# Attention and a gated two-layer product on one core: offsets for the first three chunks, 16 float32 heads instead of 24, the weights' checks near the end, the gate written over h

## The chip, the cores and the metric

The kernel runs on one core of a Trainium2 chip. The metric is the time of one execution on the device in microseconds (us); lower is better. PE is TensorE, which multiplies matrices; DVE (VectorE), ACT (ScalarE) and POOL (GpSimd) work element by element; SP issues the DMA transfers. PSUM is the memory that PE writes, in banks of 128 x 512 float32 values; SBUF is the other memory on the chip.

## What is computed

```python
# q, k, v: (4, 8, 768, 64) float32; n_sink = 4, window = 128
scores = (1 / sqrt(64)) * q @ k.T
keep = (pos_k < n_sink) | ((pos_q - pos_k >= 0) & (pos_q - pos_k < window))
scores = where(keep, scores, -1e9)
a = exp(scores - max(scores)); a = a / (sum(a) + 1e-9)
x = concat_heads(a @ v)                # 3072 x 512
h = x @ w_in                           # w_in 512 x 2048
out = (h * cos(h)) @ w_out             # w_out 2048 x 512, out 3072 x 512 float32
```

The two weights come as float64 arrays; everything else is float32. The inputs are random; q and k are scaled so that the softmax is sharp.

## The kernel before

**Tiles.** The 3072 rows are worked in 12 chunks of 256 rows: a chunk is one batch and two blocks of 128 positions, (batch, first block). Each chunk has 8 heads, and after them 8 slots. A slot takes 256 of the 2048 columns of h.

**Numbers in pieces.** A product of nearly float32 accuracy is made of three products of a shorter type (float32r): each operand is kept as a high part and a low rest, and hi*hi, lo*hi and hi*lo are summed in PSUM. The weights are turned from float64 into such pieces on the chip at the start (weight_piece: 32 pieces of 512 KB; three integer steps on DVE, L482, L488, L494, the high part on ACT, L515, the rest on DVE or POOL, L518).

**A slot** (dense): 24 h matmuls of 128 x 256 (L381) into one PSUM bank; then ACT scales h into an integer number of turns (L390), DVE takes the rest of the turn (L396, tile r), ACT the cosine (L403), DVE multiplies h and the cosine, the gate (L408, into r), ACT takes the high part ghi (L414) and DVE or POOL the low rest glo (L420). After that, 12 acc matmuls of 128 x 512 (L429) add the slot's part to the chunk's two output banks. After a chunk's last slot the output is copied through a raw buffer (L370, L372) and stored. r, ghi and glo have two buffers each; h goes round over the banks b4 and b2 in the first two chunks, and over b4, b2 and b3 from the third.

**A head.** The first NEH = 24 heads, three chunks of 8, are "early" and take the float32 path: q and k are loaded in natural order and turned on PE (L713), scores are float32 matmuls (L737), the values too (L925), and a small matmul (L327) takes the high part of x away again. The other heads take the split path: q and k are loaded in strips and turned on DVE (L695, L766), split by ACT and DVE or POOL (l: L753, L760; k: L778, L784), and scores (L793) and values (L949) are float32r matmuls. Both paths share the masks on DVE (L806), the exponent on ACT (L815), the denominator (L824, L825), the norm of p (L835 on DVE or POOL, L833 on ACT), and the turn of p on PE (L895) with its high and low part (L904, L911). Chunks that don't begin at block 0 also see the sink columns: they have 264 instead of 256 score columns and some extra small steps (L865, L867, L877). The early chunks are the first chunks of batches 0, 1 and 2, so with NEH = 24 the chunks come as (0,0), (1,0), (2,0), (0,2), (0,4), (1,2) and so on.

**Checks.** The integer steps hold only for weights that aren't tiny. So all 32 pieces are loaded again later (check_piece), and DVE takes the least square of each (L533); at the end one value, redo, decides whether a general path runs, which it doesn't here. A check shares the two buffers raw and the two buffers wt with the weights, and raw with the output copies. Before, each slot from the third chunk on adds one check, with a priority of CK = 27.4 us after the slot's time.

**What sets the order.** Every step is handed to a list scheduler (Plan.order), with its engine or engines, its model duration, what it needs, and a priority in us that comes from the time of its head or slot plus constants of the table C. The scheduler runs through model time and on each engine takes the ready step of the lowest priority; where a step may go to several engines, constants such as POOLPEN and POOLF weigh them. The result is a fixed order for each engine, written out in the program; nothing is decided on the chip. A buffer's next use waits for the users of its last one.

Of the kernel before, what the change touches and what calls it, by code (L numbers as in the profile page):

```python
# [172 lines left out]
def attn_moe_kernel(ctx, tc, q, k, v, n_sink, window, w_in, w_out, out):  # L173
# [232 lines left out]
    def gate(o):  # L406
        def fn(e):
            nc.vector.tensor_tensor(out=o.r, in0=o.h, in1=o.r, op=ALU.mult)  # L408
        return fn

    def g_hi(o):
        def fn(e):
# [1 line left out]
            nc.scalar.copy(out=o.ghi, in_=o.r)  # L414
        return fn

    def g_lo(o):
        def fn(e):
# [1 line left out]
            e.tensor_tensor(out=o.glo, in0=o.r, in1=f32(o.ghi), op=ALU.subtract)  # L420
# [123 lines left out]
    def dense(plan, x, a, s, t, T, w_in_ready, w_out_ready, acc_banks, h_bank):  # L544
# [8 lines left out]
        if True:  # L553
# [13 lines left out]
            a0 = add([("ACT", act(FG * NT, False))], turns(o), mm + [by], t + C["DM"] + 7.2)  # L567
            a2 = add([("DVE", dve(FG * NT))], rest(o), [a0, br], t + C["DM"] + 8.0)
# [1 line left out]
            a3 = add([("ACT", act(FG * NT) + 0.09)], cosine(o), [a2], t + C["DM"] + 8.9, table="sin")  # L570
            a4 = add([("DVE", dve(FG * NT))], gate(o), [a3], t + C["DM"] + 9.5)
# [840 lines left out]
```

## Time and profile before

| | |
|---|---|
| three runs | 771.24, 774.18, 778.17 us |
| median | 774.18 us |
| profiled execution, its own time | 773.9 us |
| its span in the trace | 772.1 us |
| mean granted PE clock | 0.993 |
| instructions | 15308 |
| DMA, the kernel's transfers | 70.43 MB, mean busy share of 16 engines 38.2% |

The profiled execution is 0.3 us from the median, and 1.8 us longer than its span. The prediction shows the lines of the page and of the trace. In them, "x" is a count; a chain row has start, duration and what ran; a group row has the line, engine, operation, tiles, shapes, then busy us, mean ns of one, and the idle time ahead of them with what ended it.

### The profile page before, as it was taken

To read this page: it belongs to the slowest core of one execution; us is meant where nothing else is said; L and a number is where in the kernel's file an instruction comes from. 1 tells how busy PE (TensorE), PEld (TensorE's weight loads), DVE (VectorE), ACT (ScalarE), POOL (GpSimd) and SP (SyncE) were. 2 spreads that over 40 slices of the span, in tenths; PEclk is the share of its full clock that TensorE was granted. 3 is DMA by queue.
4 is the path that set the end of the run, shared out by engine and by line. 5 is a ranking of instruction groups with operands and counts; after the bars stand their busy time and mean duration, and the time that the engine had idled before them with its cause. 6 is when DMAs were issued, how large, how long until landed. Compare 5 with 4: busy or idle time off the path is not lost.

```text
span 772.1 us, 15308 instructions
## 1 busy us (share of the span) xinstructions
PE 748.2 (97%) x4987; PEld 660.9 (86%) x4987; DVE 608.5 (79%) x1597; ACT 577.9 (75%) x1345; POOL 150.5 (19%) x233
## 2 busy tenths in 40 slices
PE   7899999999989999999999999999999999999996
PEld 6566777888978989888899999999999999999995
DVE  6868888778868889989989988888878988964432
ACT  2779796878868787787787887897798788784332
POOL 2122210100313432212234321210211221220000
PEclk9999999999999999999999999999999999999998
DMA  5655464332455366275367243232242233110000
GB/s 149 173 158 170 133 192 156 65 57 39 88 157 110 56 185 163 40 191 138 65 164 187 45 114 54 46 70 45 38 87 53 46 76 60 31 39 1 28 1 32
DMA packets 215673, 71.50 MB, mean 93 GB/s; under 512 B 204320, under 2 KB 204320, under 8 KB 215584
## 3 DMA queue, kind: packets, MB, share of 16 engines
q1 hardware_dynamic: 215584, 70.43, 38.2%
q8 instruction: 41, 0.67, 0.4%
q14 instruction: 48, 0.39, 0.2%
HBM read 64.10 MB, written 6.29 MB: 91 GB/s over the span
## 4 chain that ended last, share of the span: by engine, by line
PE 80%; DVE 7%; DMA 5%; ACT 4%; issue 2%; SPq 1%; DVEq 0%; ACTq 0%
PE h L381 31%; PE acc L429 29%; PE av L949 5%; PE tp L895 4%; PE s L793 4%; DMA raw<-in_moe_w_in_dram 3%; PE s L737 2%; PE av L925 2%; DMA xk<-in_k_dram 1%; ACT p L815 1%; PE gp L877 1%; DVE p L806 1%; DVE plo L911 1%; DVE r L396 1%; SPq L675 1%
## 5 line engine op out<-in xcount | busy, mean ns | idle before, releaser
L381 PE MATMUL h<-xhi,whi_in 128*128 128x256 f32 x768 | 224.0, 292 | 2.4 <-DVE r L408 2.4
L381 PE MATMUL h<-xlo,whi_in 128*128 128x256 f32 x768 | 217.2, 283 | 0.1
L381 PE MATMUL h<-xhi,wlo_in 128*128 128x256 f32 x768 | 216.9, 282 | 0.0
L381 PEld LDWEIGHTS h<-xhi,whi_in 128*128 128x128 f32 x768 | 145.8, 190 | 15.3 <-issue 4.5
L429 PE MATMUL acc<-whi_out,ghi 128*128 128x512 f32 x384 | 157.5, 410 | 0.0
L381 PEld LDWEIGHTS h<-xhi,wlo_in 128*128 128x128 f32 x768 | 146.1, 190 | 7.5
L429 PE MATMUL acc<-wlo_out,ghi 128*128 128x512 f32 x384 | 151.7, 395 | 0.0
L429 PE MATMUL acc<-whi_out,glo 128*128 128x512 f32 x384 | 150.5, 392 | 0.0
L381 PEld LDWEIGHTS h<-xlo,whi_in 128*128 128x128 f32 x768 | 145.8, 190 | 0.3 <-DVE xlo L337 0.3
L806 DVE CUSTOM_DVE_ANT_0 p<-s,mk 128x264 f32<-128x264 f32 (+1 forms) x192 | 76.8, 400 | 33.2 <-PE s L793 21.8
L815 ACT ACTIVATE p<-p,st 128x264 f32<-128x264 f32 (+1 forms) x192 | 93.4, 489 | 0.7
L403 ACT ACTIVATE r<-r,neg 128x512 f32<-128x512 f32 x96 | 69.0, 723 | 26.7 <-DVE r L396 24.3
L429 PEld LDWEIGHTS acc<-whi_out,glo 128*128 128x128 f32 x384 | 72.2, 188 | 16.5
L420 DVE TENSOR_TENSOR glo<-r,ghi 128x512 fp32r<-128x512 f32 x82 | 57.7, 703 | 31.3 <-ACT ghi L414 30.5
L414 ACT CAST ghi<-r 128x512 fp32r<-128x512 f32 x96 | 59.0, 615 | 30.0 <-PE acc L429 29.0
L429 PEld LDWEIGHTS acc<-whi_out,ghi 128*128 128x128 f32 x384 | 72.6, 189 | 5.0 <-issue 0.7
L429 PEld LDWEIGHTS acc<-wlo_out,ghi 128*128 128x128 f32 x384 | 73.0, 190 | 3.8 <-DVE wlo_out L518 0.3
L408 DVE TENSOR_TENSOR r<-h,r 128x512 f32<-128x512 f32 x96 | 65.2, 680 | 11.7 <-ACT r L403 11.4
L390 ACT ACTIVATE yt<-h 128x512 int32<-128x512 f32 x96 | 57.1, 595 | 18.1 <-PE h L381 16.0
L396 DVE SCALAR_TENSOR_TENSOR r<-h,yt 128x512 f32<-128x512 f32 x96 | 65.6, 683 | 5.4 <-ACT yt L390 4.0
L835 POOL TENSOR_SCALAR p<-p,st 128x264 f32<-128x264 f32 (+2 forms) x65 | 36.7, 576 | 156.3 <-DVE st L825 122.3
L848 POOL TENSOR_TENSOR vr<-v,vr 128x192 fp32r<-128x192 f32 (+1 forms) x59 | 34.9, 591 | 160.6 <-ACT vr L843 143.2
(128 smaller groups left out, 1392.8 us busy)
## 6 DMA issues: line engine op xcount, KB each, us to landing
raw<-in_moe_w_in_dram SPq DMA_DIRECT2D x32, 512.0 KB
raw<-in_moe_w_out_dram SPq DMA_DIRECT2D x32, 512.0 KB
xk<-in_k_dram SPq DMA_DIRECT2D x256, 48.0 KB
out_dram<-raw SPq DMA_DIRECT2D x24, 256.0 KB
v<-in_v_dram SPq DMA_DIRECT2D x64, 96.0 KB
xq<-in_q_dram SPq DMA_DIRECT2D x144, 32.0 KB
v<-in_v_dram SPq DMA_DIRECT2D x32, 64.0 KB
xq<-in_q_dram SPq DMA_DIRECT2D x24, 64.0 KB
```

What stands on the lines that cost most here:

```text
L381: nc.tensor.matmul(out=o.h[:, t, :], lhsT=w[:, c, fs], rhs=xx[:, c, :], start=(c == 0 and n == 0), stop=(c == NC - 1 and n == 2),)
L390: nc.scalar.activation(out=yt, in_=o.h, func=AF.Copy, scale=INV2PI, bias=0.25)
L396: nc.vector.scalar_tensor_tensor(out=o.r, in0=o.h, scalar=INV2PI, in1=yt, op0=ALU.mult, op1=ALU.subtract)
L403: nc.scalar.activation(out=o.r, in_=o.r, func=AF.Sin, scale=TWOPI_DOWN, bias=quarter)
L408: nc.vector.tensor_tensor(out=o.r, in0=o.h, in1=o.r, op=ALU.mult)
L414: nc.scalar.copy(out=o.ghi, in_=o.r)
L420: e.tensor_tensor(out=o.glo, in0=o.r, in1=f32(o.ghi), op=ALU.subtract)
L429: nc.tensor.matmul(out=x.acc[j], lhsT=gg[:, t, j * P : (j + 1) * P], rhs=w[:, f, :], start=(f == 0 and n == 0), stop=(f == NFT - 1 and n = ...
L806: nc.vector.tensor_tensor_reduce(out=o.p[:, j, :w], in0=o.s_ps[j][:, :w], in1=masks[min(o.i0 + j, 2)][:, :w], op0=ALU.add, op1=ALU.min, sc ...
L815: nc.scalar.activation(out=o.p[:, j, :w], in_=o.p[:, j, :w], func=AF.Exp, bias=o.lead.st[:, 0, o.nth, j : j + 1], scale=-1.0, accum_out=o. ...
L835: e.tensor_scalar(out=o.p[:, j, :w], in0=o.p[:, j, :w], scalar1=r, scalar2=1.0, op0=ALU.mult, op1=ALU.mult)
L949: nc.tensor.matmul(out=dst, lhsT=lhs, rhs=rhs, start=(n == 0), stop=(n == len(seq) - 1), skip_group_check=True)
```

## The change

Seven things change. The constants of C have new values (one line is shown). NEH is 16, so that the third chunk is now (0,2), on the split path and with sinks, and (2,0) comes later, on the split path too; with two early chunks the h banks are two in the first chunk only and three from the second. FIRST gives the steps of the first three chunks offsets of their own by kind of step (h, acc, the middle of a slot, q and k, scores, exponent, v, values), and the weights' pieces a shift by slot. The gate writes over h in PSUM, ghi and glo read it there, glo runs on DVE alone, r is free after the gate and the bank after glo. Checks are added so that they all end with the last slot: CR = 0.876 a slot in the last 8 slots, CS = 0.643 a slot before those. The idle matmuls that fill PE's waits at the start are 40 instead of 60. A minus of an odd head waits for the first part of its pair.

```diff
-    "DV": 4.41, "DX": 7.018, "FILL": 60, "GHI": 2, "GLO": 2, "L": 1, "LAG": 4.21, "LEAD": 18.263, "NEH": 24,
+    "LEAD": 24.62, "NEH": 16, "NM": 2.964, "NW": 2.34, "NWF": 0.132, "PB": 5, "PEN": 21.472, "PL": 3, "POOLF": 0.59,
...
+FIRST = {
+    "A": [-1.28, 4.17, 0.42], "H": [-6.37, 2.87, -2.13], "L": [-3.51, 18.2, 4.58], "M": [4.02, -1.74, 1.96],
...
+    def extra(kind, a):
+        return FIRST[kind][a] if a < 3 else 0.0
...
-            m = add([("PE", 0.11)], x_minus(x, p, odd), [i], t + 0.3)
+            m = add([("PE", 0.11)], x_minus(x, p, odd), [i] + (x.parts[p][:1] if odd else []), t + 0.3)
...
-            nc.vector.tensor_tensor(out=o.r, in0=o.h, in1=o.r, op=ALU.mult)
+            nc.vector.tensor_tensor(out=o.h, in0=o.h, in1=o.r, op=ALU.mult)
...
-            nc.scalar.copy(out=o.ghi, in_=o.r)
+            nc.scalar.copy(out=o.ghi, in_=o.h)
...
-            e.tensor_tensor(out=o.glo, in0=o.r, in1=f32(o.ghi), op=ALU.subtract)
+            e.tensor_tensor(out=o.glo, in0=o.h, in1=f32(o.ghi), op=ALU.subtract)
...
-            bh.users += [a0, a2, a4]
-            a5 = add([("ACT", act(FG * NT))], g_hi(o), [a4, bhi], t + C["DM"] + 10.2)
-            a6 = add(sub(FG * NT), g_lo(o), [a5, blo], t + C["DM"] + 10.8, port=True)
-            br.users += [a5, a6]
+            br.users.append(a4)
+            a5 = add([("ACT", act(FG * NT, False))], g_hi(o), [a4, bhi], tm + 10.2)
+            a6 = add([("DVE", dve(FG * NT))], g_lo(o), [a5, blo], tm + 10.8)
+            bh.users += [a0, a2, a4, a5, a6]
...
-            if a > 1 and len(checked) < len(checks):
+            left = len(slots) - nh
+            while len(checked) < len(checks) - C["CR"] * min(left, NSLOT) - C["CS"] * max(left - NSLOT, 0):
                 checked.append(check_piece(plan, t + C["CK"], len(checked), checks[len(checked)][2]))
```

The order that the scheduler writes moves throughout. Slots are counted from 0 through the whole run: 0 to 7 are the first chunk's. In the rows below, a name holds the slot (h_11, r_9, glo_8) or the batch, the first block and the head (p_0_2_2), and a number that only tells tiles apart; lines behind the table have moved by 6 to 10.

Early in PE's order, where slot 6 of the first chunk (counted from 0) begins, before:

```order
L327 MATMUL av_1_0_6_1113<-xhi_1_759,gt_80 64x256
L737 MATMUL s_2_0_4_1_1196<-tk_2_0_4_1159,tq_2_0_4_1154 128x256
L713 MATMUL qk_2_0_6_1200<-ident_79,xq_74 128x128 x2
L713 MATMUL qk_2_0_6_1200<-ident_79,xk_75 128x128 x2
L381 MATMUL h_6_1215<-xhi_0_405,whi_in_89 128x256
L381 MATMUL h_6_1215<-xhi_0_405,wlo_in_90 128x256
```

And after:

```order
L803 MATMUL s_0_2_2_1_1211<-r1_0_2_2_1130,l_0_2_2_1127 128x264
L803 MATMUL s_0_2_2_1_1211<-r2_0_2_2_1172,l_0_2_2_1127 128x264
L935 MATMUL av_1_0_6_1158<-pt_1_0_7_1175,v32_1_77 64x256
L935 MATMUL av_1_0_6_1158<-pt_1_0_7_1175,v32_1_77 64x128
L336 MATMUL av_1_0_6_1158<-xhi_1_750,gt_80 64x256
L390 MATMUL h_8_1032<-xhi_1_750,whi_in_89 128x256
L390 MATMUL h_8_1032<-xhi_1_750,wlo_in_90 128x256
L390 MATMUL h_8_1032<-xlo_1_764,whi_in_89 128x256
L390 MATMUL h_6_1248<-xhi_0_416,whi_in_89 128x256
```

The float32 scores and turns of (2,0) are gone, split scores of (0,2) stand in their place, and slot 8, of the second chunk, begins ahead of slot 6, in the third bank.

DVE around the point at which the bank of slot 11 comes free. Before, that is the gate of slot 9:

```order
L420 TENSOR_TENSOR glo_7_1502<-r_7_1372,ghi_7_1492 128x512
L518 TENSOR_TENSOR wlo_out_92<-wt1_73,whi_out_91 128x512
L482 TENSOR_SCALAR wt0_72<-raw0_70 128x512
L396 SCALAR_TENSOR_TENSOR r_9_1524<-h_9_1417,yt_81 128x512
L488 SCALAR_TENSOR_TENSOR wt0_72<-raw0_70,wt0_72 128x512
L806 ISA p_2_0_7_1536,st_2_0_4_1183<-s_2_0_7_0_1515,mk_173 128x128
L806 ISA st_2_0_4_1183 128x1
L494 SCALAR_TENSOR_TENSOR wt0_72<-raw0_70,wt0_72 128x512
L482 TENSOR_SCALAR wt1_73<-raw1_71 128x512
L408 TENSOR_TENSOR r_9_1524<-h_9_1417,r_9_1524 128x512
```

After, it is glo of slot 8:

```order
L417 TENSOR_TENSOR h_9_1414<-h_9_1414,r_9_1513 128x512
L405 SCALAR_TENSOR_TENSOR r_10_1617<-h_10_1535,yt_81 128x512
L776 STREAM_TRANSPOSE tk_0_2_7_1625<-xk_75 128x3x128
L491 TENSOR_SCALAR wt1_73<-raw1_71 128x512
L875 CAST gc_186<-p_0_2_2_1196 128x2x8
L875 CAST gc_186<-p_0_2_3_1312 128x2x8
L877 TENSOR_TENSOR gc_186<-p_0_2_2_1196,gc_186 128x2x8
L877 TENSOR_TENSOR gc_186<-p_0_2_3_1312,gc_186 128x2x8
L497 SCALAR_TENSOR_TENSOR wt1_73<-raw1_71,wt1_73 128x512
L429 TENSOR_TENSOR glo_8_1653<-h_8_1032,ghi_8_1627 128x512
```

The turns of k, the sink columns and the rest of slot 10 have come in ahead of the step that frees the bank, and that step is now a glo.

DVE where the checks stand. Before, beside the slots of the third chunk and the heads of the fourth, (0,2):

```order
L420 TENSOR_TENSOR glo_18_2548<-r_18_2396,ghi_18_2538 128x512
L396 SCALAR_TENSOR_TENSOR r_20_2554<-h_20_2467,yt_81 128x512
L533 ISA wt0_72,tiny_87<-raw0_70 128x512
L533 ISA tiny_87 128x1
L533 ISA wt1_73,tiny_87<-raw1_71 128x512
L533 ISA tiny_87 128x1
L824 TENSOR_SCALAR st_0_2_4_1987<-st_0_2_4_1987 128x8
L825 RECIPROCAL st_0_2_4_1987<-st_0_2_4_1987 128x8
L835 TENSOR_SCALAR p_0_2_4_1986<-p_0_2_4_1986,st_0_2_4_1987 128x264 x2
```

After, the last of them, beside the last slots:

```order
L542 ISA wt0_72,tiny_87<-raw0_70 128x512
L542 ISA tiny_87 128x1
L417 TENSOR_TENSOR h_92_9898<-h_92_9898,r_92_9958 128x512
L542 ISA wt1_73,tiny_87<-raw1_71 128x512
L542 ISA tiny_87 128x1
L405 SCALAR_TENSOR_TENSOR r_93_10009<-h_93_9949,yt_81 128x512
L542 ISA wt0_72,tiny_87<-raw0_70 128x512
L542 ISA tiny_87 128x1
L429 TENSOR_TENSOR glo_92_10022<-h_92_9898,ghi_92_10007 128x512
L417 TENSOR_TENSOR h_93_9949<-h_93_9949,r_93_10009 128x512
```

The checks have moved from the middle of the run to its second half, and the norms of p that stood behind them on DVE are on POOL or ACT in the whole order of after.

More of the change, by code (lines that the diff above doesn't have):

```diff
@@ L562, in dense @@
                     mm.append(
-                        add([("PE", 0.655)], h_mm(o, x, tt, half), d + mm[-1:], t + C["DH"] + (3.5, 5.8)[tt] + 0.6 * half)
+                        add([("PE", 0.655)], h_mm(o, x, tt, half), d + mm[-1:], t + C["DH"] + extra("H", a) + (3.5, 5.8)[tt] + 0.6 * half)
                     )
@@ L566, in dense @@
             x.blo.users += mm
[L567 to L568 removed]
+            tm = t + C["DM"] + extra("M", a)
+            a0 = add([("ACT", act(FG * NT, False))], turns(o), mm + [by], tm + 7.2)
+            a2 = add([("DVE", dve(FG * NT))], rest(o), [a0, br], tm + 8.0)
             by.users.append(a2)
[L570 to L575 removed]
+            a3 = add([("ACT", act(FG * NT) + 0.09)], cosine(o), [a2], tm + 8.9, table="sin")
+            a4 = add([("DVE", dve(FG * NT))], gate(o), [a3], tm + 9.5)
+            br.users.append(a4)
+            a5 = add([("ACT", act(FG * NT, False))], g_hi(o), [a4, bhi], tm + 10.2)
+            a6 = add([("DVE", dve(FG * NT))], g_lo(o), [a5, blo], tm + 10.8)
+            bh.users += [a0, a2, a4, a5, a6]
             for tt in range(FG):
@@ L1052, in before_softmax @@
                     oo.bl = buf("l", C["L"])
-                    q1 = add([("ACT", act(NT))], q_hi(o, oo), [q0, oo.bl], t - 6 * T + C["DQ"] + 0.6)
-                    oo.ql = add([("DVE", dve(NT))], q_lo(o, oo), [q1], t - 6 * T + C["DQ"] + 0.9, port=True)
+                    q1 = add([("ACT", act(NT))], q_hi(o, oo), [q0, oo.bl], t - 6 * T + dq + 0.6)
+                    oo.ql = add([("DVE", dve(NT))], q_lo(o, oo), [q1], t - 6 * T + dq + 0.9, port=True)
                     btq.users += [q1, oo.ql]
@@ L1142, in after_softmax @@
             bav = buf("av", 1)
-            p0 = add([("PE", 0.107 * o.n)], turn(o), o.nm + [pt], t + C["DA"] + 1.3)
+            p0 = add([("PE", 0.107 * o.n)], turn(o), o.nm + [pt], t + da + 1.3)
             o.bp.users.append(p0)
-            p1 = add([("ACT", act(o.n * P, False))], p_hi(o), [p0, bhi], t + C["DA"] + 1.8)
-            p2 = add([("DVE", dve(o.n * P))], p_lo(o), [p1, blo], t + C["DA"] + 2.3)
+            p1 = add([("ACT", act(o.n * P, False))], p_hi(o), [p0, bhi], t + da + 1.8)
+            p2 = add([("DVE", dve(o.n * P))], p_lo(o), [p1, blo], t + da + 2.3)
             pt.users += [p1, p2]
@@ L1151, in after_softmax @@
                 deps += oe.sinks
-            y0 = add([("PE", 0.5)], values(o), deps, t + C["DA"] + 4.0)
+            y0 = add([("PE", 0.5)], values(o), deps, t + da + 4.0)
             for bb in (bvr, bhi, blo):
@@ L1158, in after_softmax @@
             bxb = buf("xb", 1)
-            y1 = add([("ACT", act(NT, False))], x_low(o), [y0, bxb], t + C["DA"] + 4.8)
+            y1 = add([("ACT", act(NT, False))], x_low(o), [y0, bxb], t + da + 4.8)
             if o.odd == 0:
                 x.bf = buf("x", 1)
-            y2 = add([("DVE", dve(NT))], x_sum(o, x), [y0, y1] + (x.sums[o.pair] or [x.bf]), t + C["DA"] + 5.1)
+            y2 = add([("DVE", dve(NT))], x_sum(o, x), [y0, y1] + (x.sums[o.pair] or [x.bf]), t + da + 5.1)
             bav.users += [y1, y2]
@@ L1166, in after_softmax @@
             if o.odd:
-                x.bf.users += split_x(plan, x, o.a, o.pair, t + C["DA"] + 5.4)
+                x.bf.users += split_x(plan, x, o.a, o.pair, t + da + 5.4)
         idle = buf("b1", 1)
```

75 lines of the change are left out of this document (39 added, 36 removed).

## The prediction

> **What bounds the kernel now.** I read the page's totals and the shares of the chain that ended last, then busy time by stretches of the run, then the chain itself, then single events.
>
> ```profile
> PE 748.2 (97%) x4987; PEld 660.9 (86%) x4987; DVE 608.5 (79%) x1597; ACT 577.9 (75%) x1345; POOL 150.5 (19%) x233
> PE 80%; DVE 7%; DMA 5%; ACT 4%; issue 2%; SPq 1%; DVEq 0%; ACTq 0%
> ...
> core 0: us, PE busy (x) PEld busy (x) DVE busy (x) ACT busy (x) POOL busy (x), PEclk, DMA share, GB/s
> 0.00:40.00 40.00, 33.02 (x178) 25.05 (x179) 28.48 (x102) 19.86 (x60) 7.22 (x18) 0.96 0.59 159
> 40.00:80.00 40.00, 38.11 (x214) 26.90 (x215) 30.76 (x82) 33.53 (x94) 9.16 (x10) 1.00 0.56 158
> 80.00:137.20 57.20, 54.70 (x319) 42.34 (x318) 49.09 (x109) 42.55 (x91) 7.54 (x8) 1.00 0.53 159
> 137.20:200.00 62.80, 62.80 (x405) 54.32 (x404) 47.79 (x124) 51.41 (x112) 6.84 (x12) 1.00 0.30 57
> 200.00:380.00 180.00, 174.62 (x1217) 158.90 (x1216) 155.66 (x417) 144.00 (x339) 49.15 (x72) 0.99 0.51 123
> 380.00:700.00 320.00, 320.00 (x2271) 295.53 (x2270) 271.67 (x728) 262.92 (x615) 70.62 (x114) 1.00 0.34 71
> 700.00:772.10 72.10, 64.98 (x397) 57.81 (x396) 25.05 (x40) 23.60 (x38) 0.00 (x0) 0.97 0.05 16
> ```
>
> The first line says PE, but PE's ends are modelled, so 97% is not PE at its peak. The stretches say more: from 380 to 700 us PE has no gap at all, and what it loses it loses before 137 us, between 200 and 380 us, and at the end. To price that, I take PE's pace from the chain where PE is full:
>
> ```profile
> 712.43 1.39 PE acc L429 x6
> 713.82 1.43 PE h L381 x12
> ```
>
> An h matmul is 1.43/12 = 0.119 us, an acc matmul 1.39/6 = 0.232. A slot (24 h, 12 acc) is 2.86 + 2.78 = 5.64 us, 96 slots 541 us. The attention's matmuls at their full-stretch pace (rows below) add 160. So the span is 701 us of work and 71 us of loss. Loss at a point of the run is the clock less the work handed over by then, and h11 (the fourth slot of the second chunk) is where the start ends:
>
> ```profile
> 117.18 0.69 DVE L408 TENSOR_TENSOR r<-h,r 128x512 f32<-128x512 f32 x1 [0.19 <-ACT r L403]
> 117.93 0.39 PE L381 MATMUL h<-xhi,whi_in 128*128 128x256 f32 x1 [0.93 <-DVE r L408]
> ...
> 137.19 0.69 DVE L408 TENSOR_TENSOR r<-h,r 128x512 f32<-128x512 f32 x1 [0.20 <-ACT r L403]
> ...
> 141.17 0.28 PE L381 MATMUL h<-xhi,whi_in 128*128 128x256 f32 x1
> ```
>
> The first pair is h8: PE waits for the gate of slot 6, which frees the PSUM bank, and begins 0.06 us after its end. Ahead of h11 the order has 264 h matmuls (31.4 us), 84 acc (19.5) and attention for 43.3: 94.2 of work at 141.2 us, a loss of 47. By the same count the loss is 49 at 179 us, 61 at 420, 64 at 750, and 7 more go at the end. So 47 of 71 us are lost at the start, where DVE's chain (weights, masks, gates) holds the banks, and about 12 between 179 and 420.
>
> **8 heads fewer in float32.** The heads of the third batch's first chunk go over to the split path. What the two paths do alike on PE (the turns of p) drops out.
>
> ```profile
> 20.84 0.41 PE s L737 x2
> ...
> 28.01 0.80 PE av L925 x4
> 28.81 0.85 PE s L737 x4
> 29.66 0.37 PE qk L713 x2
> ...
> 32.69 0.26 PE av L327
> ...
> 40.81 0.22 PE qk L713 x2
> ...
> 544.24 0.17 PE s L793 x2
> ...
> 547.59 0.24 PE s L793 x2
> 548.54 0.36 PE av L949 x4
> ```
>
> A float32 head, by the slow rows: scores 0.85, values 0.80, turns of q and k 0.37, minus 0.26 = 2.28 us. By the quick rows, scores are 0.41 for the wide part and half of that for the narrow, 0.62, and turns 0.22: 1.90. A split head: 0.17 + 0.24 + 0.36 = 0.77. Saved: 8 x 1.13 = 9 to 8 x 1.51 = 12. I take -9, the quick rows, since these heads stood after 100 us where PE is nearly full. Range -12 to -8.
>
> **The start.** The third chunk is now (batch 0, block 2), already on the split path and with sinks, so its preparation goes to DVE where PE did it. Ahead of h11 PE has 16 turns of q and k, 8 heads' scores, 3 heads' values and 3 minus fewer, and 6 heads' split scores and 2 heads' split values more: by the rows above 5 us less, 89. But h11 sits on the third bank, which slot 8 held, and that is now free only once glo has read it (the gate is written over h). So I compare DVE's queue up to glo of slot 8 with that up to the gate of slot 9 before.
>
> ```profile
> L408 DVE TENSOR_TENSOR r<-h,r 128x512 f32<-128x512 f32 x96 | 65.2, 680 | 11.7 <-ACT r L403 11.4
> L420 DVE TENSOR_TENSOR glo<-r,ghi 128x512 fp32r<-128x512 f32 x82 | 57.7, 703 | 31.3 <-ACT ghi L414 30.5
> ...
> L911 DVE TENSOR_TENSOR plo<-tp,phi 128x512 fp32r<-128x512 f32 x64 | 43.7, 683 | 1.9 <-ACT phi L904 1.3
> L766 DVE STREAM_TRANSPOSE tk<-xk 128x384 f32<-128x384 f32 x64 | 36.2, 566 | 1.2 <-DMA xk<-in_k_dram 0.7
> ...
> L760 DVE TENSOR_TENSOR l<-tq,l 64x256 fp32r<-64x256 f32 x72 | 32.1, 445 | 5.5 <-ACT l L753 3.3
> ...
> L695 DVE STREAM_TRANSPOSE tq<-xq 128x256 f32<-128x256 f32 x36 | 15.6, 432 | 0.6 <-DMA xq<-in_q_dram 0.4
> ```
>
> More in the queue: 8 turns of k (4.5), 4 of q (1.7), 6 l (2.7), 2 plo (1.4), 3 glo (2.1), a gate and a rest (1.4), some 25 small ones netted (2.6): 16 us by their durations. Each instruction's record begins a little before the one ahead ends; in the first 137.2 us the durations sum to 126 while DVE is busy for 108.3 (28.5 + 30.8 + 49.1). So 16 are 14 of queue. DVE idles 28.9 us in that stretch, 17.3 of it after 40 us. If it idles as before, h11 comes at 138 + 14 = 152; if all idle time after 40 us fills up, DVE is ready at 135 and PE sets it, 136 = 141 - 5. The idle is there because DVE waits for PE and ACT, and with a longer queue part of that closes; I take the middle, 145. Loss there 145 - 89 = 56 instead of 47: +9, range 0 to +16.
>
> Behind h11 the float32 scores that stood between h11 and h16 are gone and three banks go round instead of two; only 2 us were lost there, so -2, range -4 to 0.
>
> **The gate over h.** Its duration can only be bounded: gate now writes PSUM, ghi and glo read it. The lower end is the row nearest in kind, plo, which reads PSUM and a copy (0.683), the upper glo as it was (0.703): 96 x 0.02 = 2 us of DVE either way. I take nothing, since DVE has gaps past the start. Glo also loses POOL: 14 glo go to DVE, 14 x 0.70 = 10 us of DVE, counted in the queues above and below. R comes free a step earlier, and the bank a step later; past the start glo ends well before the third slot behind it needs the bank, 5.64 us each.
>
> [...]
>
> **Checks moved, norms to POOL.** Before, one check per slot came in slots 16 to 47, between 180 and 380 us; now from slot 49 on, seven of them in the last five slots.
>
> ```profile
> 214.14 5.92 DMA raw<-in_moe_w_in_dram
> ...
> 220.08 0.69 DVE wt L533
> ...
> 221.14 0.37 DVE p L835
> 221.65 1.10 PE tp L895 x4
> ...
> L533 DVE CUSTOM_DVE_ANT_0 wt<-raw 128x512 f32<-128x512 f32 x32 | 25.3, 790 | 9.4 <-DMA raw<-in_moe_w_in_dram 5.8 <-DMA raw<-in_moe_w_out_dram 3.4
> ...
> L835 DVE TENSOR_SCALAR p<-p,st 128x264 f32<-128x264 f32 x53 | 20.8, 448 | 0.4
> ...
> L835 POOL TENSOR_SCALAR p<-p,st 128x264 f32<-128x264 f32 x49 | 27.9, 582 | 89.6 <-DVE st L825 77.7 <-ACT ghi L414 7.7 <-PE acc L429 4.3
> ```
>
> This is the wait that cost PE there: a check's load lands late, DVE stands before the check (9.4 us in all), the norm of p queues behind it, and PE's turn of p behind that. Of the 12 us lost from 179 to 420, some 2 would be lost at the later pace (3 in 330 us); 10 are to be had at most. All norms leave DVE (75 to none; POOL 65 to 137), so DVE's work from gate 16 to gate 48 falls by 23 us (durations less overlap), while from gate 48 to gate 88 it is the same within 2 us in spite of the checks. I take -6, range -10 to 0: the checks' loads can land late at their new place too, but the norms no longer queue behind them on DVE. A norm on POOL takes 0.58 instead of 0.45, 0.13 later for PE's turn, whose head is scheduled slots ahead. In the last five slots DVE is busy 25 of 72 us, so seven checks of 0.87 fit; if the last loads hold a raw buffer that the output copies need, it costs up to 5. SP issues 32 transfers more and is not on the chain beyond 1%. For all these: 0, range 0 to +5.
>
> **Sum.** The profiled execution took 773.9 us (span 772.1), the median of three runs is 774.2, so they agree. 773.9 - 9 + 9 - 2 - 6 = 765.9, forecast 766.
>
> **Rivals.** (a) DVE's idle time closes and PE sets h11 at 136 with the old loss of 47; the start costs nothing and the rest comes whole or better: 773.9 - 9 - 2 - 8 = 755. For it: DVE is idle 29 us of 137. Against: the queue holds instructions that wait for ACT and loads.
> (b) The checks make the same waits where they now stand, so that moving them does nothing: 773.9 - 9 + 9 - 2 = 772. For it: a load of 512 KB that takes 5.9 us at 214 us may take as long later, and the two raw buffers are the same. Against: DMA's share is 0.34 there and not 0.51.
> (c) Slower: glo holds h11's bank while DVE's queue waits for the longer chain ghi, glo; idle grows by 5 us, and h11 comes at 157, loss 68: +21; late heads reach into the next stretch and leave half of the checks' gain: 773.9 - 9 + 21 - 2 - 3 = 781. It decides from h11 at about 150 to 153, where the other terms are used up. For it: PE waited for the gate there already. Against: before, the third chunk's float32 work stood on PE in the same place.
>
> **Chances.** The forecast's case .35 (758 to 772, somewhat more than half of it below 766.4), (a) .25, (b) .22, (c) .14, others .04. About 1% is what a measurement of this kernel can tell from no change: bounds 766.4 and 781.9. Faster: .20 + .25 = .45. Slower: .10 of (c) and .02 of the others = .12. Same: .15 + .22 + .04 + .02 = .43. The range takes in (a) but for .06 and (b), and leaves out .10 of (c) and the others, .20 in all: 752 to 778.
>
> **What would show it.** The start of h11: 136 speaks for (a), 145 for the forecast, 155 for (c). A wait of PE's h for DVE's glo shows the bank. Between 200 and 380 us PE should have no gap and the turns of p no wait for the norm; a DVE wait for the check's load after 480 us speaks for (b) if PE waits in the same place. The chain from 400 us on should have the same 1.43 and 1.39 pieces. Wrong altogether I would be if PE's pace itself changed, or the end after 750 us grew by more than 5.

## The result, and the profile after

The changed kernel takes 788.22 us (median of 4 runs, 783.94 to 791.44), the kernel before 776.17 in the same comparison (median of 4): a ratio of 1.0155, with a 95% interval of 1.0112 to 1.0197. It is slower, outside the range, and 7 us above even the slow rival (c), 781. The profiled execution took 785.7 us (before: 773.9), so the sum below is against +11.8.

The page of the changed kernel, its totals and the shares of the chain that ended last:

```profile
PE 748.6 (96%) x4943; PEld 664.8 (85%) x4943; DVE 596.1 (76%) x1547; ACT 565.7 (72%) x1350; POOL 196.0 (25%) x336
...
PE 77%; ACT 7%; DVE 6%; DMA 5%; issue 3%; POOL 0%; SPq 0%; DVEq 0%; ACTq 0%; POOLq 0%
```

DVE and ACT have 12 us less to do than before, POOL 45 more, PE by its modelled ends the same, and the span is 11.8 us longer. The stretches of the changed kernel (length, busy time and instructions of each engine, granted clock, DMA share, GB/s), with the third one now reaching to the start of h11:

```profile
0.00:40.00 40.00, 32.03 (x136) 23.12 (x136) 25.46 (x90) 15.95 (x48) 9.17 (x21) 0.74 0.56 151
40.00:80.00 40.00, 36.06 (x153) 23.86 (x152) 27.90 (x76) 25.37 (x69) 6.47 (x9) 0.75 0.52 142
80.00:160.20 80.20, 67.59 (x399) 57.02 (x399) 68.76 (x153) 55.16 (x129) 24.55 (x31) 0.94 0.54 140
160.20:200.00 39.80, 39.74 (x278) 36.44 (x279) 32.94 (x85) 29.88 (x69) 10.03 (x18) 1.00 0.29 57
200.00:380.00 180.00, 179.41 (x1272) 164.58 (x1272) 142.32 (x378) 150.31 (x363) 52.12 (x91) 1.00 0.32 60
380.00:700.00 320.00, 317.16 (x2221) 290.91 (x2220) 261.08 (x692) 254.51 (x606) 88.28 (x157) 1.00 0.42 95
700.00:783.90 83.90, 76.61 (x492) 68.91 (x490) 37.62 (x79) 34.55 (x70) 5.34 (x10) 0.98 0.21 68
```

Two things are to be seen. DVE was busy for 122.1 us before h11 (25.5 + 27.9 + 68.8) and idle for 38.1; before, up to the gate of slot 9 at 137.2, it was busy for 108.3 and idle for 28.9. And the clock column, which the prediction's sum has no term for, is 0.74 and 0.75 in the first 80 us, where it was 0.96 and 1.00.

The start of h11 in the changed kernel, in the timeline (start, duration, engine, what; in brackets the wait ahead of it):

```profile
146.14 0.70 DVE L417 TENSOR_TENSOR h<-h,r 128x512 f32<-128x512 f32 x1 [0.43 <-ACT r L412]
...
156.99 0.59 ACT L423 CAST ghi<-h 128x512 fp32r<-128x512 f32 x1 [0.23 <-PE acc L438]
...
159.53 0.68 DVE L429 TENSOR_TENSOR glo<-h,ghi 128x512 fp32r<-128x512 f32 x1
...
160.26 0.39 PE L390 MATMUL h<-xhi,whi_in 128*128 128x256 f32 x1 [1.15 <-DVE glo L429]
```

The gate of slot 8 is done at 146.8, but its bank is held until glo has read it, at 160.2. Between them ghi waits for PE's acc: there are two ghi buffers, and the one that slot 8 needs is free only after the acc matmuls of slot 6. So a bank now waits for an accumulation two slots older, on top of DVE's queue.

By the prediction's own count, loss is the start of a slot less the work handed over by then. "By slot 16" is the point at which PE begins its 385th h matmul, that is, after 16 slots of 24; 48 and 88 likewise. "PE work" is counted with the prediction's pitches, not measured:

| profiled execution | loss by slot 16 | 16 to 48 | 48 to 88 | behind | PE work | sum |
|---|---|---|---|---|---|---|
| before | 179.3 - 130.1 = 49.2 | 11.9 | 3.1 | 7.2 | 700.7 | 772.1 |
| changed | 200.3 - 128.4 = 71.9 | 3.9 | 8.0 | 7.4 | 692.7 | 783.9 |

All that was lost is lost in the start: +22.7. PE has 8 us less to do, the middle gained 8.0, the later stage gave 4.9 back.

### The profile page after: what moved, and what is told of

It reads as the page before. It is cut to its first block, busy times and chain, and to the rows that moved or that the text cites. A ratio compares the mean times of both kernels' runs of the same rounds, so it can differ in the third digit from the quotient of the medians.

```text
span 783.9 us, 15346 instructions
## 1 busy us (share of the span) xinstructions
PE 748.6 (96%) x4943; PEld 664.8 (85%) x4943; DVE 596.1 (76%) x1547; ACT 565.7 (72%) x1350; POOL 196.0 (25%) x336
## 4 chain that ended last, share of the span: by engine, by line
PE 77%; ACT 7%; DVE 6%; DMA 5%; issue 3%; POOL 0%; SPq 0%; DVEq 0%; ACTq 0%; POOLq 0%
PE h L390 31%; PE acc L438 28%; PE av L959 5%; PE tp L905 4%; PE s L803 4%; ACT p L825 2%; DMA xq<-in_q_dram 2%; PE s L747 2%; PE av L935 1%; DMA xk<-in_k_dram 1%; DMA raw<-in_moe_w_in_dram 1%; PE gp L887 1%; ACT r L412 1%; DVE glo L429 1%; DVE wt L497 1%
## 5 line engine op out<-in xcount | busy, mean ns | idle before, releaser
L390 PE MATMUL h<-xhi,whi_in 128*128 128x256 f32 x768 | 227.9, 297 | 4.7 <-DVE glo L429 4.6
L390 PEld LDWEIGHTS h<-xhi,whi_in 128*128 128x128 f32 x768 | 147.7, 192 | 14.6 <-DVE glo L429 5.9
L438 PE MATMUL acc<-whi_out,ghi 128*128 128x512 f32 x384 | 155.5, 405 | 0.0
L390 PEld LDWEIGHTS h<-xhi,wlo_in 128*128 128x128 f32 x768 | 148.1, 193 | 5.0
L858 POOL TENSOR_TENSOR vr<-v,vr 128x192 fp32r<-128x192 f32 (+1 forms) x77 | 45.7, 594 | 277.0 <-ACT vr L853 244.7
L845 POOL TENSOR_SCALAR p<-p,st 128x264 f32<-128x264 f32 (+2 forms) x137 | 65.5, 497 | 81.5 <-DVE st L835 56.4
L417 DVE TENSOR_TENSOR h<-h,r 128x512 f32<-128x512 f32 x96 | 66.2, 691 | 19.6 <-ACT r L412 19.3
L429 DVE TENSOR_TENSOR glo<-h,ghi 128x512 fp32r<-128x512 f32 x96 | 65.6, 684 | 14.2 <-ACT ghi L423 13.9
L803 PE MATMUL s<-r,l 128*128 128x264 f32 (+2 forms) x320 | 65.5, 285 | 2.7 <-DVE st L816 2.0
```

Source lines behind the costliest of these rows:

```text
L390: nc.tensor.matmul(out=o.h[:, t, :], lhsT=w[:, c, fs], rhs=xx[:, c, :], start=(c == 0 and n == 0), stop=(c == NC - 1 and n == 2),)
L417: nc.vector.tensor_tensor(out=o.h, in0=o.h, in1=o.r, op=ALU.mult)
L429: e.tensor_tensor(out=o.glo, in0=o.h, in1=f32(o.ghi), op=ALU.subtract)
L438: nc.tensor.matmul(out=x.acc[j], lhsT=gg[:, t, j * P : (j + 1) * P], rhs=w[:, f, :], start=(f == 0 and n == 0), stop=(f == NFT - 1 and n = ...
L803: nc.tensor.matmul(out=o.s_ps[j][:, :w], lhsT=o.l[:, j * P : (j + 1) * P], rhs=r.rearrange("p n s -> p (n s)")[:, c0 : c0 + w], start=(n = ...
L845: e.tensor_scalar(out=o.p[:, j, :w], in0=o.p[:, j, :w], scalar1=r, scalar2=1.0, op0=ALU.mult, op1=ALU.mult)
```

## The experiments

The parts of the change were first tried alone in the kernel before, and undone alone in the changed one; then the numbers (constants, offsets, idle matmuls). Each time is a median with the ratio to the kernel before in the same comparison. "Loss" is that of the profiled execution, as above, and "clock" its granted clock from 24 to 48 us. A name with b_ is made from the kernel before, one with a_ from the changed one. The loss is that of one execution and the time a median, and executions of one kernel differ by several us (the changed kernel's four by 7.5), so a difference of a few us in one column needs the other beside it.

| run | time, us | ratio (95%) | clock | loss by 16 | 16 to 48 | 48 to 88 |
|---|---|---|---|---|---|---|
| before | | 1 | 1.00 | 49.2 | 11.9 | 3.1 |
| changed | 788.2 | 1.0155 (1.0112-1.0197) | 0.53 | 71.9 | 3.9 | 8.0 |
| b_neh16 | 777.4 | 1.0022 (0.9990-1.0053) | 1.00 | 67.8 | 9.1 | 4.1 |
| b_gate_h | 776.4 | 1.0008 (0.9981-1.0035) | 1.00 | 54.0 | 7.6 | 4.4 |
| b_checks | 771.1 | 0.9970 (0.9945-0.9996) | 1.00 | 48.7 | 2.2 | 9.0 |
| bc_fill80 | 771.4 | 0.9965 (0.9929-1.0001) | 1.00 | 49.5 | 3.1 | 7.5 |
| b_drop20 | 777.6 | 1.0020 (0.9984-1.0056) | 0.79 | 52.8 | 11.1 | 3.5 |
| a_oldC | 775.0 | 1.0017 (0.9987-1.0047) | 1.00 | 61.7 | 3.8 | 6.6 |
| a_gate_r | 783.3 | 1.0127 (1.0086-1.0167) | 0.52 | 65.4 | 3.9 | 9.1 |
| a_first0 | 783.8 | 1.0123 (1.0078-1.0168) | 0.51 | 64.7 | 3.4 | 12.1 |
| a_neh24 | 796.9 | 1.0274 (1.0185-1.0364) | 0.79 | 57.1 | 10.5 | 12.8 |
| a_neh24_gr | 784.5 | 1.0121 (1.0071-1.0171) | 0.51 | 63.8 | 2.2 | 8.3 |
| a_checks | 789.4 | 1.0186 (1.0149-1.0223) | 0.53 | 72.1 | 8.4 | 8.2 |
| a_fill60 | 786.9 | 1.0120 (1.0082-1.0157) | 0.57 | 69.1 | 3.9 | 8.6 |
| a_fill100 | 773.2 | 0.9952 (0.9917-0.9987) | 1.00 | 62.0 | 2.8 | 8.9 |
| a_fill140 | 782.3 | 1.0088 (1.0060-1.0117) | 1.00 | 66.8 | 3.2 | 8.5 |
| a_f100_drop60 | 781.3 | 1.0060 (1.0025-1.0096) | 0.52 | 69.0 | 2.8 | 7.9 |
| a_idle1 | 789.0 | 1.0160 (1.0075-1.0244) | 0.79 | 71.6 | 4.0 | 9.7 |
| a_idle3 | 790.2 | 1.0179 (1.0134-1.0224) | 1.00 | 73.7 | 3.9 | 10.7 |
| a_gr_f0_fill100 | 779.3 | 1.0051 (1.0010-1.0093) | 1.00 | 61.6 | 4.0 | 7.2 |

### Idle matmuls and heads

**One idle matmul behind each PE step, in the changed kernel's own order.** (a_idle1)

```diff
...
+            if seen == int(C["FILL"]) and st[3] == "PE" and not hasattr(st[2], "fill"):
+                more += [(st[0], st[1], fill(1), "PE")] * 1
...
```

> The changed kernel with its own order on every engine, and 41 idle matmuls more: one behind each PE step between the last of its 40 idle matmuls and the first h. Clock theory (PE waited long enough around 18 to 24 us for its clock to fall to 0.50, which doubled its work up to 46 us): the clock stays near 1.0 from 16 to 50 us, the first h begins at 42 to 45 us instead of 50.0, and the time falls by 5 us or more, to 783 or less. DVE theory (the start is set by DVE's longer queue, and the slow clock only fills PE's waiting): the clock recovers, but the fourth slot of the second chunk still begins at 157 us or later, and the time stays within 2 us of 788. If neither, the idle matmuls cost up to 41 x 0.12 = 5 us.

Measured: 789.0. The first h came at 55.1, not earlier, and slot 11 at 160.0. In its profile the clock was low already from 16 to 32 us (0.61), so the run doesn't tell the clock from the rest.

**The last 20 idle matmuls left out of the kernel before**, its order kept. (b_drop20)

```diff
+            fn.fill = n
...
-        emit(steps)
+        emit([st for st in steps if getattr(st[2], "fill", 0) < 40])
```

> The kernel before with its own order on every engine, and the last 20 of its 60 idle matmuls left out. Clock theory: the granted clock falls to 0.5 somewhere between 20 and 50 us, the fourth slot of the second chunk begins 5 to 12 us later than 141, and the time rises by 5 to 12 us, to 781 to 788. DVE theory: the clock may fall, but the time rises by less than 3 us.

Measured: 777.6, a ratio whose interval holds 1. The clock did fall, to 0.50 and for ten us only, in this kernel's stretches:

```profile
16.00:24.00 8.00, 6.83 (x40) 4.63 (x39) 6.75 (x27) 4.06 (x15) 0.00 (x0) 1.00 0.46 132
24.00:34.00 10.00, 9.39 (x31) 5.79 (x31) 6.41 (x21) 6.69 (x23) 1.58 (x2) 0.50 0.56 153
34.00:48.00 14.00, 13.40 (x73) 8.40 (x71) 9.81 (x33) 11.11 (x33) 3.69 (x6) 0.99 0.64 174
```

It cost 3.6 us of loss by slot 16 in the profile. Why the clock came back here after ten us, and only after some 23 in the changed kernel (0.50 from 23 to 46 us), no run shows.

**FILL, the number of idle matmuls, at 60 in the changed kernel**, planned anew. (a_fill60)

```diff
-    "FILL": 40
+    "FILL": 60
```

> The changed kernel with the constant FILL at 60 again, the order planned anew with it. Clock theory: as with the added idle matmuls, the clock holds past 24 us and the time falls by 5 us or more. DVE theory: within 2 us of 788.

Measured: 786.9, the DVE theory's number. But the clock held only some four us longer and was then low up to 47 us (0.68 from 24 to 32 us, 0.50 from 32 to 40, 0.54 from 40 to 48): twenty more only move the gap, and the run doesn't tell the two theories apart.

**16 float32 heads alone, in the kernel before.** (b_neh16)

```diff
-    "NEH": 24
+    "NEH": 16
```

> The kernel before with 16 float32 heads instead of 24 alone; all other constants, 60 idle matmuls among them, as before, the order planned anew. If the third chunk on the split path by itself makes the start late (more DVE work, less PE work ahead of the second chunk's end, so also less to keep PE's clock up): the fourth slot of the second chunk begins at 150 us or later, and the time is above 776 in spite of 9 us less PE work. If the loss is in the idle matmuls and the offsets: that slot begins by 145 us, and the time is 765 to 772.

Measured: 777.4, no difference to before. Slot 11 began at 154.5 and the loss by slot 16 rose by 18.6 in the profiled execution, which took 783.0 us and had its clock down early (0.60 from 16 to 24 us, 1.00 from 24 to 48). So the 8 us of PE work that the split path saves are taken back in the time, and the start is later; how much later with the clock up, this profile doesn't say.

### The bank and the checks

**The gate back in r, in the changed kernel.** (a_gate_r)

```diff
-            nc.vector.tensor_tensor(out=o.h, in0=o.h, in1=o.r, op=ALU.mult)
+            nc.vector.tensor_tensor(out=o.r, in0=o.h, in1=o.r, op=ALU.mult)
...
-            bh.users += [a0, a2, a4, a5, a6]
+            bh.users += [a0, a2, a4]
+            br.users += [a5, a6]
...
```

> The changed kernel with the gate written into r again, so that a bank is free after the gate and glo may run on POOL; everything else as changed, the order planned anew. In the trace of the changed kernel the gate of slot 8 ends at 146.8, its glo at 160.2, and the fourth slot of the second chunk begins at 160.3. Bank theory: that slot begins at 150 to 156, the loss there falls by 4 us or more, and the time falls to 784 or less. Queue theory (DVE's queue is late whoever frees the bank): it begins at 158 or later, and the time is 786 to 790.

Measured: 783.3, and 6.5 less loss by slot 16: the bank theory's numbers, but for the slot, which began earlier still (147.3). By the medians the bank costs the changed kernel about 5 us. That isn't clear of noise: the ratio is 1.0127 (1.0086 to 1.0167), the changed kernel's 1.0155 (1.0112 to 1.0197).

**The checks back at their old place, in the changed kernel.** (a_checks)

```diff
-            while len(checked) < len(checks) - C["CR"] * min(left, NSLOT) - C["CS"] * max(left - NSLOT, 0):
+            if a > 1 and len(checked) < len(checks):
...
```

> The changed kernel with the weights' checks where they were: one per slot from slot 16 on, CK 27.435; everything else as changed, planned anew. If moving the checks gained what was forecast (6 us): the time rises by 4 to 8, to 791 to 796. If the same waits only came later (the changed kernel loses 4 us from slot 16 to 48 instead of 12, but 8 from slot 48 to 80 instead of 2.6): the loss moves back to slots 16 to 48, and the time is within 2 us of 787.5.

Measured: 789.4, within the 2 us of the second theory; the middle lost 8.4 again instead of 3.9. But the loss between slots 48 and 88 did not go down with it (8.2, against 8.0 with the checks there), although the last check now stands at 468 us, some five slots behind slot 48. So in the changed kernel the checks are not shown to be what costs there.

**The gate over h alone, in the kernel before**, b_gate_h (the three statements of the diff, glo on DVE, the bank's users).

```diff
...
-            bh.users += [a0, a2, a4]
...
+            bh.users += [a0, a2, a4, a5, a6]
```

> The kernel before with the gate over h alone: ghi and glo read PSUM, glo on DVE only, the bank free after glo; planned anew with the constants of before. Bank theory: with two banks in the first two chunks every slot there waits for the glo of the slot two before, the fourth slot of the second chunk begins at 146 or later, and the time rises by 4 us or more, to 780 or more. If the gate's place costs nothing: within 2 us of 776.5.

Measured: 776.4, no difference. The loss by slot 16 rose by 4.8 in the profile, of which 1.8 is left by slot 88. In the kernel before, the bank costs nothing that the time shows.

**The checks alone, moved in the kernel before.** (b_checks)

```diff
...
-            if a > 1 and len(checked) < len(checks):
+            left = len(slots) - nh
+            while len(checked) < len(checks) - 0.876 * min(left, NSLOT) - 0.643 * max(left - NSLOT, 0):
```

> The kernel before with the checks alone at their new place (0.643 a slot before the last 8 slots, 0.876 in them, CK 18.531); planned anew with the constants of before. If the checks' waits vanish at the new place: the time falls by 4 to 8, to 768 to 773. If they only come later: within 2 us of 776.5, with loss of 5 or more between slot 48 and 80.

Measured: 771.1, 0.3% less (0.04 to 0.55). The middle lost 2.2 instead of 11.9, the later stage 9.0 instead of 3.1: the wait goes, and more than half of it comes back later.

### Undoing two parts, and the offsets

**24 float32 heads in the changed kernel.** (a_neh24)

```diff
-    "NEH": 16
+    "NEH": 24
```

> The changed kernel with 24 float32 heads again, so that the third chunk is (2,0) in float32 as before; everything else as changed, planned anew. With 16 heads, before lost 18 us more by slot 16 and had 8 us less PE work. Chunk theory (the third chunk's split path is the larger part of the late start): the loss at slot 16 falls from 72 to 60 or less, and the time, with 8 us of PE work more, to 784 or less. If the offsets and the bank make the start late whatever the third chunk is: the loss at slot 16 stays at 66 or more, and the time is above 790.

Measured: the start as the chunk theory says (57.1), but 796.9 in all, with 10.5 and 12.8 lost later on. Neither theory has that time. Why so much is lost later was not followed up, and the time says nothing about the chunk.

**24 heads and the gate in r.** (a_neh24_gr)

```diff
-    "NEH": 16
+    "NEH": 24
...
-            nc.vector.tensor_tensor(out=o.h, in0=o.h, in1=o.r, op=ALU.mult)
+            nc.vector.tensor_tensor(out=o.r, in0=o.h, in1=o.r, op=ALU.mult)
...
```

> The changed kernel with 24 float32 heads and the gate written into r, planned anew: both parts that cost the start are undone; the offsets, the other constants, 40 idle matmuls and the checks' new place stay. If these two are the cause: the loss at slot 16 is 49 to 54, and the time 768 to 775, as with the checks alone moved. If the offsets and the 40 idle matmuls cost more by themselves: 778 or more, with the clock below 0.6 between 24 and 48 us.

Measured: 784.5, with the clock at 0.51. With both parts undone the start still loses 63.8, so the numbers cost by themselves: the kernel before with the checks moved, b_checks, has much the same parts with the old numbers, and its ratio is 0.9970 against 1.0121 here.

**No offsets in the changed kernel.** (a_first0)

```diff
-        return FIRST[kind][a] if a < 3 else 0.0
+        return 0.0
...
```

> The changed kernel with all offsets of the first three chunks and of the weights' pieces at zero, planned anew. If the offsets make the first h late (50 us instead of 40) and the clock low: the first h begins by 44 us, the clock from 24 to 48 us is above 0.8, and the time falls by 3 us or more, to 784 or less. If they help the start that the third chunk makes late: the time rises by 3 us or more, to 790 or more. Within 2 us of 787.5: they do neither.

Measured: 783.8, as the first theory says of the time, but not by its way: the first h came at 51.7 and the clock was 0.51. What is gained is behind that (slot 11 at 153.2), and 4.1 of it is lost again between slots 48 and 88. Here too the ratio, 1.0123 (1.0078 to 1.0168), is not clear of the changed kernel's.

**80 idle matmuls with the checks moved, in the kernel before.** (bc_fill80)

```diff
-    "FILL": 60
+    "FILL": 80
...
```

> The kernel before with the checks at their new place and 80 idle matmuls instead of 60, planned anew. Executions of before at a mean clock of 0.995 take about 772, at 0.988 about 776. Clock theory: more idle matmuls keep the clock up in more executions, so the median clock is 0.994 or more and the median time 768 to 770, against 771 with 60. If the spread of the clock doesn't come from the start: the same spread as with 60, 770 to 775, or slower by the 2 us that 20 idle matmuls may take.

Measured: 771.4, as with 60. The kernel before has enough of them.

### Numbers or parts

**The changed code with the old constants** and no offsets; of the new numbers only 16 heads and the checks' place. (a_oldC)

```diff
...
-    "DQ": 11.83, "DS": -3.724, "DV": 4.174, "DX": 8.466, "FILL": 40, "GHI": 2, "GLO": 2, "L": 1, "LAG": 3.127,
+    "DV": 4.41, "DX": 7.018, "FILL": 60, "GHI": 2, "GLO": 2, "L": 1, "LAG": 4.21, "LEAD": 18.263, "NEH": 16,
...
```

> The changed kernel's code with the constants of before (60 idle matmuls among them) and no offsets; of the new numbers only 16 float32 heads, the checks' new place (CK, CR, CS) stay; planned anew. It has all structural parts: the third chunk on the split path, the gate over h, the checks late. If the time comes from these parts (16 heads alone 0 to +2, gate alone 0 to +1, both on the same bank +6, checks alone -5): 776 to 780, with a loss of 65 or more at slot 16 and the clock above 0.8 from 24 to 48 us. If the new constants and offsets are harmless, it is as slow as the changed kernel, 785 to 790. If the parts are harmless together with the old constants: 770 or less.

Measured: 775.0, a little under what was expected of the parts. 12.5 us more are lost by slot 16 and 8 us less work is done; 8.1 are gained in the middle and 3.5 given back: -0.1 together. All parts of the code together are worth nothing either way; the constants and offsets make the 12 us. Up to the start of h11, at 153.4, DVE was busy for 129.0 us and idle for 24.4:

```profile
0.00:153.40 153.40, 129.53 (x729) 100.91 (x730) 128.99 (x329) 105.19 (x263) 33.61 (x47) 0.94 0.56 150
```

**100 idle matmuls in the changed kernel**, planned anew. (a_fill100)

```diff
-    "FILL": 40
+    "FILL": 100
```

> The changed kernel with 100 idle matmuls, which the plan now places up to the last steps ahead of the first h; planned anew, all else as changed. Clock theory: no gap is left for the clock to fall from 24 to 48 us (0.53 with 40, 0.55 with 60 idle matmuls), the first h begins at 42 or earlier, and the time is 782 or less. If DVE's queue sets slot 11 whatever the first h does: the clock is up, the first h early, slot 11 still at 157 or later, and the time 785 to 789.

Measured: 773.2, faster than before by 0.5% (0.1 to 0.8). One constant, with the order that is planned with it, takes back 15 us. The stretches of this kernel, the last one up to its h11:

```profile
16.00:24.00 8.00, 8.00 (x55) 6.62 (x54) 6.21 (x18) 3.55 (x12) 0.00 (x0) 1.00 0.53 157
24.00:48.00 24.00, 23.32 (x132) 16.01 (x131) 16.23 (x53) 17.02 (x55) 8.90 (x13) 1.00 0.60 159
0.00:150.50 150.50, 132.76 (x746) 104.00 (x746) 121.22 (x311) 97.20 (x245) 44.20 (x60) 0.93 0.57 152
```

**The gate in r, no offsets and 100 idle matmuls.** (a_gr_f0_fill100)

```diff
-    "FILL": 40
+    "FILL": 100
...
-        return FIRST[kind][a] if a < 3 else 0.0
+        return 0.0
...
-            nc.vector.tensor_tensor(out=o.h, in0=o.h, in1=o.r, op=ALU.mult)
+            nc.vector.tensor_tensor(out=o.r, in0=o.h, in1=o.r, op=ALU.mult)
...
```

> The changed kernel with the gate in r, no offsets and 100 idle matmuls, planned anew: of the numbers the other constants, of the parts the third chunk's split path and the checks' place are left. Gate in r alone gave 783.3, no offsets alone 783.8. If these two and the clock are separate costs of 4 us each and more: 770 to 776. If they are the same wait counted twice, 780 to 784.

Measured: 779.3, between the two theories. Bank, offsets and clock don't add up; with the clock up, undoing the other two makes it worse (1.0051, 1.0010 to 1.0093, against 0.9952, 0.9917 to 0.9987).

**The order that was planned with 100, and 60 of them left out.** (a_f100_drop60)

```diff
+            fn.fill = n
...
-        emit(steps)
+        emit([st for st in steps if getattr(st[2], "fill", 0) < 40])
```

> The kernel planned with 100 idle matmuls, its order kept on every engine, and the last 60 of them left out, so that 40 are left as in the changed kernel. With 100 the time is 773.2 and the clock 1.00 from 16 to 48 us. Clock theory: the clock falls to 0.5 from about 24 us, and the time rises by 8 us or more, to 781 to 789. If the gain came from the other order that was planned with them: within 3 us of 773.

Measured: 781.3, the clock theory's number. Every other instruction stands where it stood, so the 8 us between this and 773.2 are the idle matmuls and what they do to the clock (1.00 from 24 to 48 us with them, 0.52 without). The ratios are clear of each other (1.0060, 1.0025 to 1.0096, against 0.9952, 0.9917 to 0.9987). The other 7 us, from 788.2 to 781.3 with 40 idle matmuls in both, go with the order that was planned; what in it, no run shows. The stretches of this run:

```profile
16.00:24.00 8.00, 6.74 (x40) 4.74 (x39) 7.36 (x23) 3.37 (x11) 0.00 (x0) 1.00 0.55 165
24.00:48.00 24.00, 22.41 (x68) 13.17 (x69) 13.78 (x42) 13.44 (x46) 6.95 (x10) 0.52 0.48 128
0.00:157.50 157.50, 135.93 (x686) 102.55 (x686) 121.93 (x311) 97.69 (x246) 43.61 (x60) 0.84 0.52 145
```

In the second row PE is nearly as busy as with 100 (22.4 against 23.3 us, which has idle matmuls in it), at a clock of 0.52, and DVE gets 2.5 us less done. The third row goes up to h11: DVE has the same 311 instructions behind it as with 100 (121.9 and 121.2 us), but was idle for 35.6 us instead of 29.3.

**Three idle matmuls behind each step, in the changed kernel's own order.** (a_idle3)

```diff
...
+            if seen == int(C["FILL"]) and st[3] == "PE" and not hasattr(st[2], "fill"):
+                more += [(st[0], st[1], fill(1), "PE")] * 3
...
```

> The changed kernel with its own order on every engine, and three idle matmuls behind each PE step between the last of its 40 and the first h, 123 in all (one behind each gave 789.0, with the clock at 0.61 from 16 to 32 us in its profile). Clock theory: the clock stays at 0.9 or above from 16 to 48 us in most executions and the time falls to 774 to 780. If only the new plan helps: 785 or more.

Measured: 790.2, a miss. Its stretch from 24 to 48 us has the clock at 1.00 and DVE hardly busier than in the changed kernel (13.1):

```profile
24.00:48.00 24.00, 23.75 (x145) 18.23 (x144) 13.91 (x43) 13.57 (x47) 6.38 (x9) 1.00 0.42 113
```

By an estimate, 123 matmuls take 15 us at 0.12, the pitch of an h matmul of the same 128x256 in the kernel before (1.43 us for 12); they stand behind every step and not only where PE waits, and the first h came at 56.4 instead of 50.0. So in the changed kernel's own order no run shows a gain from the clock by itself: what the added matmuls cost can't be told from what the clock gives.

**140 idle matmuls in the changed kernel**, planned anew. (a_fill140)

```diff
-    "FILL": 40
+    "FILL": 140
```

> The changed kernel with 140 idle matmuls, planned anew, so that they reach past the first h. With 100 the clock is still 0.50 to 0.73 from 56 to 72 us, and the fourth slot of the second chunk begins at 150.5. Clock theory: the dip from 56 to 72 us goes, that slot begins by 147, and the time is 768 to 772. If DVE's queue sets the rest: 772 to 776.

Measured: 782.3, outside both theories. The clock is 1.00 from 16 to 72 us, but the idle matmuls now stand between the first slots too, and the loss by slot 16 is 4.8 above that with 100. More isn't better here.

## Why the prediction was wrong

**8 heads fewer in float32**, -9: right, at the small end of its range. The work, counted by the same pitches, fell from 700.7 to 692.7.

**The start**, +9 with h11 at 145: wrong, and this decides. Measured are +24 (160.3 - 88.9 = 71.4 against 47.0). Two of its three numbers were right: PE's work ahead of h11 (89 forecast, 88.9 found), and DVE's queue (14 us longer forecast, 122.1 - 108.3 = 13.8 found). The step that failed is "with a longer queue part of that closes; I take the middle". DVE's idle time did not close by 7 us, it grew by 9.2; 13.8 + 9.2 is all of the 23 us from the end of the one window (137.2) to that of the other (160.2). Of the rivals only (c) has the idle time grow, by 5 us and through ghi and glo.

The runs show where the idle time closes and where not. In the changed code with the old numbers (a_oldC) it was 24.4 us up to h11, 4.5 less than in the kernel before; there part of it did close. With the new numbers it didn't: 29.3 with 100 idle matmuls, and 35.6 with 40 in the same order, where the clock fell (0.52 from 24 to 48 us). So the wait that the prediction had wrong is DVE's wait for PE, and the term that it put at nothing is PE's clock in the first 80 us (0.74 and 0.75, where it was 0.96 and 1.00). Three things lie behind it. Only the first is clear of noise, and they overlap rather than add up:

- PE's clock. The prediction has no term for the idle matmuls. They ran out at 18 us; PE was then busy for 3.9 of the 6 us from 18 to 24, its clock fell to 0.50 at about 23 us and stayed there up to 46 us, and score and value matmuls took 1.8 to 1.9 times as long (the rows below). DVE waited 8.1 us for float32 scores between 22 and 48 us, 3.4 in the kernel before. In one and the same order, the one planned with 100, this costs 8 us (773.2 to 781.3). The change from 60 to 40 alone is not it: with 60 the changed kernel takes 786.9.
- The bank held to glo, about 5 us by the medians (a_gate_r), not clear of noise. The prediction saw that h11 needs glo of slot 8, but counted DVE's queue alone; that ghi, ahead of it, waits for an acc through its two buffers was missed; the trace shows that wait, up to 157.0.
- The offsets, about 4 us by the medians (a_first0), not clear of noise either. They were never priced. With the clock up, undoing both bank and offsets gained nothing (a_gr_f0_fill100).

The chain of the changed kernel shows the clock in two rows (start, duration, what): four score matmuls took 1.58 us, 0.85 before, and four value matmuls 1.47, 0.80 before.

```profile
28.98 1.58 PE s L747 x4
...
31.39 1.47 PE av L935 x4
```

The parts of the code together, with the old numbers, made the start 12.5 us later (a_oldC), which is above +9 and inside the term's range of 0 to +16. So +9 was a fair size for the parts; the other 10 us of the loss came from the numbers.

**Between h11 and slot 16**, -2: right. 0.5 us were lost there (71.4 to 71.9) where it had been 2.2.

**The gate over h**, 0 for DVE's durations: right. The groups of the changed kernel (busy us and mean ns behind the bar):

```profile
L417 DVE TENSOR_TENSOR h<-h,r 128x512 f32<-128x512 f32 x96 | 66.2, 691 | 19.6 <-ACT r L412 19.3
L429 DVE TENSOR_TENSOR glo<-h,ghi 128x512 fp32r<-128x512 f32 x96 | 65.6, 684 | 14.2 <-ACT ghi L423 13.9
...
L845 POOL TENSOR_SCALAR p<-p,st 128x264 f32<-128x264 f32 x96 | 46.6, 506 | 28.7 <-DVE st L835 28.7
...
L542 DVE CUSTOM_DVE_ANT_0 wt<-raw 128x512 f32<-128x512 f32 x32 | 22.1, 692 | 12.8 <-DMA raw<-in_moe_w_out_dram 8.8 <-DMA raw<-in_moe_w_in_dram 3.7
```

glo from PSUM takes 0.684, between the bounds 0.683 and 0.703.

**Checks and norms**, -6: the middle gained 8.0, as part of the range, but 4.9 came back between slots 48 and 88, so together they make -3. In the kernel before, where the move was tried alone, this is rival (b) in part: the later loss rose from 3.1 to 9.0 with it, and the move is worth 0.3%. In the changed kernel the last row above shows DVE idle for 12.8 us ahead of the checks, 12.5 of it for their loads, where it was 9.4 before; but the later loss was the same with the checks moved back (a_checks), so what makes it there stays open. A norm on POOL takes 0.506, not 0.58, and hides: 0.3 us of idle time is put down to it at the weight loads of the turns of p, none at PE's matmuls.

**The end**, 0: right, 7.4 against 7.2.

With the measured start and checks the sum is 773.9 - 8 + 24 - 1.7 - 3 = 785.2; the profiled execution took 785.7.

## What to carry to other kernels

An idle matmul that fills a wait isn't only filler: in the order planned with 100, leaving 60 out took the clock from 24 to 48 us from 1.00 to 0.52 and the time from 773.2 to 781.3. Before one is taken out, look up whether the granted clock holds where it stood, and put a term for the clock into the sum. A buffer handed on later (here a PSUM bank, to glo) inherits every wait of the steps that now hold it, so its price is read along their buffers too and not from one engine's queue: the gate of slot 8 was done at 146.8, ghi waited for an acc up to 157.0, and the bank came free at 160.2. Idle time of an engine that waits for others is not sure to close: in that same order DVE's, up to h11, was 29.3 us with the clock at 1.00 and 35.6 with it at 0.52.

Of the versions tried, the fastest are the kernel before with the checks moved (771.1, or 771.4 with 80 idle matmuls) and the changed kernel with 100 idle matmuls (773.2). Their ratios, 0.9970, 0.9965 and 0.9952, can't be told apart.
